# Two of eight feature blocks of the first token group change from eight full products to fourteen half-width ones

## The chip, the cores and the metric

The kernel runs on one core of a Trainium2 chip. Its time is the device time in microseconds (us) of one execution; the median of eight executions is given. Five engines work beside each other, each with its own queue of instructions that it takes in order: TensorE (PE in the profile, PEld its weight loads), VectorE (DVE), ScalarE (ACT), GpSimd (POOL) and the sync engine (SP), which issues most of the DMAs. They wait for each other through semaphores.

## The reference

Inputs are q, k, v of shape (8 batches, 8 heads, 576 positions, 64) and the weights w1, w2 (512 x 1024), w3 (1024 x 1024), w_out (1024 x 512), all float32.

```python
q_s = softmax of q over the last axis
k_s = softmax of k over the positions
kv  = einsum('bhsd,bhse->bhde', k_s, v)
x   = einsum('bhsd,bhde->bhse', q_s, kv)      # then (4608 tokens, 512 features)
a, b = x @ w1, x @ w2
out = ((a * b) @ w3) @ w_out                  # (4608, 512)
```

## The kernel before

**Weights.** w3 and w_out stand next to each other with nothing between them, so `make_w3o` multiplies them once (W3O, 1024 x 512), with TensorE transposes of w3. `make_w12` casts w1 and w2 to float16 in halves of 512 columns (fh 0 and 1) and also makes the combined weights `wc` that the half products need.

**Attention**, batch by batch and in two halves of four heads (i = 0, 1): exponentials of k and q on ScalarE (`ke`, `qe`), v cast (`vc`), sums and reciprocals of q's rows on VectorE (`qr`, `qi`), normalization (`qn`), transposition of q (`qt`, by TensorE with a copy `qv` for batches 0 to 3, by DMA for 4 to 7), kv on TensorE (`kv`, nine rows of 64 positions summed), its normalization on VectorE (`kn`), and x transposed (`x`), cast from PSUM to the tile `xt` (`xc`).

**The feed-forward part** takes the 4608 tokens in eight groups of 512 and 640 by turns. Its first product, a and b for eight blocks of 128 of the 1024 features, is written in one of two ways:

- `plain`: a = x w1 and b = x w2 for all tokens of the group, four products of depth 128 each (tasks `pa0`, `pa1`, `pb0`, `pb1`, two products in each). a is cast to SBUF (`pac`), and VectorE multiplies b in PSUM by it (`pm`, L664).
- `wino`: [w1, w2] and x are cut into two by two parts, with the group's tokens in halves, and seven products of parts (tasks `x1` to `x4`, `v1`, `v2`, `w`, each two matmuls over half of the tokens, L712) replace eight, as in Strassen's method in Winograd's form. The price is additions: four combinations of x for the group (`tt1` to `tt4`, L689), three snapshots of PSUM for each block (`e1` to `e3`, L385), four VectorE operations that read PSUM (`k1` to `k4`, L736; `k3` already multiplies) and one SBUF product (`k5`, L763).

Group 0 has all eight blocks `plain`, the other groups all eight `wino` (`PLAINS`, L278). The second product, `s2`, multiplies each tile of 128 tokens of a*b by W3O, eight products of 512 columns in four tasks of two (L816), each task needing two of the eight blocks. The result is evicted (`s2e`, L789 and L791) and stored (`so`, L779).

**The order** is written out by hand. Every piece of work is a task, numbered in the order in which the program adds it. `ORDER` lists the numbers in the order in which they are issued, `SLOTS` says which physical tile each buffer takes (10 staging tiles `st` for loads, 8 PSUM banks `ps`), and `ENGS` which engine does a task that has a choice. `Steps.run` (L239) goes through them; a tuple such as `('ps', 0, 11)` issues that many filler products on a blank tile (L985). An engine issues its tasks strictly in this order, and a reused tile makes a task wait for the last reader of the tile's former content. There are 28 fillers: 11, 3 and 2 among the transposes of w3, and 2, 8 and 2 around the first products of batch 0.

Of the kernel before, what the change touches and what calls it, by code (L numbers as in the profile page):

```python
# [18 lines left out]
    ('ps', 0, 11), 12, 6, 0, 1, 2, 3, 14, 120, 96, 97, ('ps', 0, 3), 72, 98, 73, 121, ('ps', 0, 2), 74, 68,  # L19
    122, 75, 80, 99, 123, 8, 81, 4, 69, 5, 82, 76, 10, 124, 128, 9, 83, 7, 84, 129, 104, 100, 130, 13, 105,  # L20
    88, 11, 131, 106, 15, 89, 132, 70, 90, 107, 108, 16, 91, 112, 17, 77, 92, 19, 125, 144, 18, 113, 85,
    142, 114, 101, 143, 109, 115, 145, 133, 71, 20, 116, 146, 147, 117, 93, 78, 140, 21, 134, 126, 135, 86,
    127, 79, 110, 136, 94, 111, 137, 102, 95, 150, 152, 22, 162, 103, 148, 164, 118, ('ps', 3, 2), 151,
    154, 163, 138, 149, 153, 139, 168, 171, ('ps', 5, 8), 155, 169, 24, 170, 23, 156, 141, 87, 119, 25,
    172, 157, 173, 165, ('ps', 2, 2), 181, 166, 158, 180, 475, 159, 160, 167, 469, 161, 481, 174, 478, 176,
    175, 472, 182, 484, 466, 183, 487, 467, 26, 479, 468, 188, 488, 470, 473, 184, 471, 190, 485, 482, 486,
    476, 502, 189, 496, 185, 503, 474, 30, 490, 191, 504, 27, 480, 497, 28, 493, 477, 194, 491, 29, 489,
    508, 31, 492, 494, 483, 1382, 495, 1396, 202, 192, 499, 204, 1397, 203, 509, 498, 505, 200, 500, 205,
    511, 510, 501, 506, 214, 1403, 507, 512, 212, 206, 1404, 513, 207, 1389, 196, 215, 1390, 197, 1398,
    213, 1391, 40, 1405, 216, 34, 193, 1392, 217, 1383, 1393, 1399, 208, 1400, 1384, 201, 209, 199, 218,  # L30
    210, 219, 1385, 198, 186, 211, 32, 222, 177, 38, 223, 179, 178, 1386, 33, 220, 224, 1406, 221, 225, 36,
    1407, 226, 229, 232, 227, 230, 1408, 228, 235, 234, 231, 533, 233, 35, 237, 518, 236, 535, 1387, 519,
    563, 514, 534, 520, 37, 515, 548, 539, 42, 516, 549, 517, 522, 521, 564, 537, 552, 536, 538, 554, 523,
    553, 567, 540, 187, 525, 541, 524, 526, 555, 542, 578, 527, 528, 568, 545, 529, 556, 530, 570, 239,
    546, 593, 531, 558, 571, 547, 565, 557, 594, 569, 559, 573, 532, 579, 543, 244, 572, 560, 195, 544,
    597, 595, 574, 598, 575, 566, 246, 582, 550, 561, 608, 583, 596, 600, 623, 551, 601, 584, 576, 624,
    599, 562, 585, 256, 247, 1417, 577, 286, 627, 602, 1410, 245, 586, 242, 605, 609, 603, 240, 606, 1411,
    587, 588, 628, 607, 580, 604, 288, 612, 581, 630, 39, 625, 248, 631, 589, 590, 249, 1409, 613, 610,
    626, 629, 238, 591, 1418, 1388, 611, 614, 41, 615, 632, 1431, 43, 592, 616, 635, 241, 1395, 617, 633,
    618, 636, 254, 1394, 620, 634, 1432, 637, 280, 1402, 621, 1412, 243, 619, 1419, 1401, 622, 255, 1433,  # L40
    284, 252, 281, 257, 1434, 253, 1424, 258, 287, 250, 1435, 259, 1425, 298, 289, 1420, 296, 264, 251,
    265, 1421, 290, 1413, 283, 285, 266, 262, 267, 282, 260, 263, 1426, 291, 261, 44, 271, 268, 272, 273,
    306, 47, 270, 269, 277, 307, 45, 278, 1414, 297, 274, 657, 275, 279, 1427, 640, 308, 276, 294, 309,
    292, 658, 295, 672, 293, 644, 638, 642, 717, 639, 1428, 659, 299, 687, 641, 643, 661, 1430, 663, 673,
    660, 646, 662, 676, 48, 645, 647, 664, 300, 648, 1415, 677, 665, 649, 301, 702, 666, 650, 667, 49, 679,
    703, 668, 669, 1416, 680, 652, 651, 678, 670, 682, 52, 688, 654, 681, 706, 1437, 671, 655, 691, 718,
    302, 683, 707, 1423, 304, 656, 653, 692, 684, 721, 303, 305, 1429, 674, 685, 704, 694, 675, 722, 709,
    705, 693, 695, 686, 689, 724, 696, 732, 690, 725, 697, 699, 733, 698, 723, 708, 710, 700, 727, 711,
    1445, 701, 726, 736, 714, 728, 737, 712, 729, 715, 325, 738, 730, 739, 310, 713, 740, 1446, 716, 312,
    741, 734, 337, 719, 311, 742, 720, 747, 744, 735, 748, 749, 731, 745, 1438, 324, 743, 751, 753, 750,  # L50
    67, 752, 1439, 754, 1440, 755, 1441, 756, 757, 746, 1442, 759, 758, 316, 313, 1444, 317, 319, 314,
    1447, 760, 315, 1436, 320, 766, 321, 781, 318, 767, 1443, 1452, 328, 762, 796, 46, 811, 782, 763, 768,
    335, 761, 1453, 769, 770, 764, 1448, 771, 329, 783, 330, 785, 773, 765, 772, 55, 784, 774, 1454, 812,
    775, 776, 786, 1455, 331, 359, 787, 778, 1456, 1449, 815, 788, 777, 1450, 1466, 789, 779, 1459, 1422,
    797, 790, 816, 798, 780, 54, 800, 323, 332, 791, 799, 1451, 333, 793, 322, 792, 818, 1457, 826, 794,
    819, 1460, 336, 801, 817, 827, 1461, 820, 358, 1462, 795, 338, 821, 50, 803, 813, 334, 822, 804, 830,
    339, 802, 814, 831, 806, 340, 1463, 823, 1467, 805, 1468, 1464, 824, 841, 807, 833, 808, 825, 834,
    1469, 341, 809, 832, 842, 856, 810, 871, 835, 857, 858, 326, 836, 859, 843, 860, 837, 872, 838, 844,
    861, 327, 847, 875, 839, 845, 876, 1473, 846, 828, 1470, 848, 829, 863, 1472, 862, 849, 877, 864, 1465,
    878, 850, 851, 879, 865, 866, 1471, 853, 840, 881, 867, 868, 854, 342, 364, 880, 855, 343, 852, 366,  # L60
    873, 344, 363, 1474, 345, 53, 883, 869, 1475, 1458, 882, 346, 870, 352, 51, 347, 874, 1480, 348, 354,
    1481, 353, 1482, 884, 920, 886, 905, 921, 907, 885, 890, 906, 888, 922, 887, 891, 1483, 908, 1476, 889,
    1484, 894, 924, 1477, 1485, 895, 909, 935, 435, 925, 923, 892, 910, 59, 897, 893, 927, 898, 896, 936,
    912, 928, 362, 899, 926, 913, 911, 929, 900, 930, 914, 950, 60, 901, 902, 951, 915, 931, 939, 62, 917,
    916, 940, 1487, 56, 903, 942, 918, 1486, 904, 954, 943, 941, 955, 937, 944, 932, 373, 945, 938, 957,
    946, 1488, 958, 933, 1489, 365, 934, 952, 947, 367, 349, 355, 919, 1490, 350, 351, 356, 965, 948, 960,
    966, 1494, 953, 357, 995, 374, 969, 996, 1495, 371, 949, 1496, 368, 970, 956, 369, 57, 967, 361, 959,
    1497, 372, 1491, 999, 962, 972, 963, 1515, 973, 961, 980, 971, 968, 370, 981, 1516, 964, 1000, 974,
    975, 1498, 984, 375, 976, 1001, 376, 1002, 1479, 977, 1003, 1508, 978, 982, 1004, 1005, 985, 997, 409,
    1006, 1007, 987, 998, 360, 1501, 377, 1008, 986, 988, 1502, 983, 402, 1503, 1009, 989, 1478, 1504, 979,  # L70
    992, 1500, 1505, 990, 993, 378, 991, 1492, 379, 994, 1493, 1517, 381, 398, 1509, 380, 403, 1510, 382,
    391, 385, 384, 383, 1518, 393, 392, 386, 1014, 387, 1044, 407, 1010, 388, 1511, 389, 390, 66, 1015,
    1029, 1011, 58, 1016, 1030, 1046, 1013, 1017, 1045, 1031, 1018, 1519, 1032, 1059, 1033, 1019, 1035,
    1012, 1034, 1522, 1512, 1047, 1048, 1021, 1513, 1049, 1020, 1022, 1036, 1514, 1523, 1023, 1037, 1050,
    396, 1507, 1038, 1039, 1051, 1040, 64, 1041, 1052, 1524, 1521, 1042, 1060, 1054, 1043, 1026, 1520,
    1053, 1063, 1074, 65, 1055, 1064, 1089, 395, 1525, 408, 1061, 1075, 1066, 1062, 1024, 1067, 1078, 1027,
    1529, 1025, 1079, 1065, 1028, 1090, 1056, 1068, 400, 1069, 1530, 1057, 1526, 1071, 61, 1070, 1081, 394,
    401, 1527, 1093, 1080, 1094, 1091, 1072, 1076, 404, 1531, 1082, 1073, 1092, 1096, 1077, 1095, 405, 410,
    1097, 1104, 1532, 1105, 1083, 1119, 1533, 1098, 1099, 1084, 1120, 1108, 1085, 1101, 1058, 1109, 406,
    1123, 1102, 436, 1086, 1536, 1087, 1103, 1124, 1537, 1100, 399, 1506, 1111, 1088, 1126, 411, 1121,  # L80
    1112, 412, 397, 1550, 1122, 1110, 1127, 1114, 431, 1113, 1543, 1115, 1129, 430, 414, 437, 413, 415,
    1544, 433, 416, 1538, 417, 432, 1499, 1106, 1125, 434, 1107, 1116, 1528, 1551, 1128, 1535, 1552, 1117,
    1130, 1131, 1118, 418, 1132, 450, 419, 451, 1133, 420, 421, 452, 1545, 423, 438, 422, 1546, 453, 1136,
    1553, 1547, 439, 424, 1554, 1168, 425, 1138, 426, 1153, 1556, 1539, 440, 1154, 1134, 63, 1183, 1169,
# [167 lines left out]
def kernel(  # L252
# [11 lines left out]
    nc = tc.nc  # L264
# [754 lines left out]
```

## Time and profile before

| what | value |
|---|---|
| median of 8 runs | 234.67 us (233.38 to 236.15) |
| the profiled execution | 234.03 us, its span 232.2 us |
| granted TensorE clock | 1.000 |
| TensorE busy | 221.1 us, 95% |
| VectorE, ScalarE, GpSimd busy | 186.8, 140.9, 90.8 us |
| HBM read, written | 38.80, 9.44 MB |

The span runs from the first to the last instruction. The first 33 us make W3O and batch 0's attention; TensorE's first product of group 0 starts at 33.4, of group 1 at 59.05, and the last product of all at 227.0. A row of a group gives the engine, the operation, what it writes and reads, its count, busy us and mean ns of one; means of operations in a run overlap, so busy divided by count is less than the mean.

### The profile page before, as it was taken

How to read it: one execution, taken by the hardware profiler on the slowest of the kernel's cores; microseconds unless marked ns; L12 is line 12 of the kernel's file. 1: busy time of each engine (PE TensorE's matmuls, PEld its weight loads, DVE VectorE, ACT ScalarE, POOL GpSimd, SP SyncE). 2: the span in 40 equal slices, each digit the busy share in tenths (PEclk: the TensorE clock that was granted, in tenths of full speed). 3: DMA queues.
4: the chain of work that ended last, by engine and by line, in shares of the span. 5: the costliest groups of instructions: out<-in, count | busy, mean ns of one | idle time of the engine just before them, and what ended most of it. 6: DMA issues, size and time to landing. Idle time of an engine off the chain costs nothing.

```text
span 232.2 us, 5571 instructions
## 1 busy us (share of the span) xinstructions
PE 221.1 (95%) x2068; PEld 134.2 (58%) x2068; DVE 186.8 (80%) x457; ACT 140.9 (61%) x306; POOL 90.8 (39%) x81
## 2 busy tenths in 40 slices
PE   7879989998999989999999999999999999999991
PEld 2544544444676558766665766656665766566640
DVE  1443695998999979989988998899988998899930
ACT  2335765556798978768745847487898843515111
POOL 3113335638268787210573535420552502210300
PEclk9999999999999999999999999999999999999999
DMA  6999999879952949948886797859664753042535
GB/s 250 380 343 389 394 387 368 295 260 350 392 190 48 332 168 324 318 130 239 234 199 136 211 326 214 167 179 273 212 99 97 200 114 76 0 90 46 118 94 134
DMA packets 32732, 50.96 MB, mean 219 GB/s; under 512 B 11712, under 2 KB 11712, under 8 KB 32704
## 3 DMA queue, kind: packets, MB, share of 16 engines
q1 hardware_dynamic: 32304, 49.95, 69.2%
q10 hardware_dynamic: 400, 0.66, 1.2%
q8 instruction: 16, 0.26, 0.5%
q14 instruction: 12, 0.10, 0.2%
HBM read 38.80 MB, written 9.44 MB: 208 GB/s over the span
## 4 chain that ended last, share of the span: by engine, by line
PE 79%; DMA 8%; DVE 7%; POOL 2%; ACT 1%; issue 1%; SPq 1%; DVEq 0%; POOLq 0%
PE ps L712 42%; PE ps L816 22%; DMA st<-in_moe_w_dram 5%; PE ps L647 5%; PE ps L418 4%; DMA st<-in_v_dram 3%; PE ps L607 2%; PE ps L562 2%; DVE eq L520 2%; DVE ds L510 1%; DVE ab L664 1%; PE ps L536 1%; POOL eq L520 1%; SPq L332 1%; PE ps L406 1%
## 5 line engine op out<-in xcount | busy, mean ns | idle before, releaser
L736 DVE TENSOR_TENSOR cc<-ps,uu 128x320 f16<-128x320 f32 (+1 forms) x168 | 71.7, 455 | 7.4 <-PE ps L712 3.7
L816 PE MATMUL ps<-W3O,ab 128*128 128x512 f16 x288 | 77.3, 379 | 0.0
L385 ACT COPY uu<-ps 128x320 f32<-128x320 f32 (+1 forms) x144 | 54.1, 406 | 36.3 <-PE ps L712 25.7
L712 PE MATMUL ps<-tt,wc 128*128 128x320 f16 (+1 forms) x336 | 57.5, 288 | 0.2 <-ACT uu L385 0.2
L712 PEld LDWEIGHTS <-wc 128*128 128x128 f16 x448 | 43.5, 98 | 19.7 <-issue 0.5
L520 POOL TENSOR_TENSOR eq<-eq,ds 128x1152 f16<-128x1152 f16 x14 | 30.1, 2147 | 34.5 <-DVE ds L517 25.9
L712 PEld LDWEIGHTS <-w 128*128 128x128 f16 x336 | 32.1, 98 | 16.6 <-issue 0.8
L712 PE MATMUL ps<-xt,w 128*128 128x320 f16 (+1 forms) x224 | 39.7, 288 | 0.0
L763 POOL TENSOR_TENSOR ab<-cc,cc 128x320 f16<-128x320 f16 (+1 forms) x27 | 20.0, 750 | 47.9 <-DVE cc L736 47.8
L816 PEld LDWEIGHTS <-ab 128*128 128x128 f16 x288 | 27.0, 98 | 18.5 <-issue 0.7
L736 DVE TENSOR_TENSOR ab<-ps,cc 128x320 f16<-128x320 f32 (+1 forms) x56 | 25.1, 454 | 1.4 <-PE ps L712 0.2
L789 ACT ACTIVATE osb<-ps 128x512 f32<-128x512 f32 x29 | 17.2, 602 | 13.8 <-PE ps L816 13.8
L385 ACT CAST xt<-ps 128x512 f16<-128x512 f32 (+3 forms) x43 | 15.0, 407 | 14.0 <-PE ps L607 14.0
L510 DVE TENSOR_REDUCE ds<-eq 128x9 f32<-128x576 f16 x32 | 23.2, 742 | 0.1
L506 ACT ACTIVATE eq<-st 128x576 f16<-128x576 f32 x32 | 21.3, 686 | 2.6 <-DMA st<-in_q_dram 2.1
L712 PE MATMUL ps<-tt,w 128*128 128x320 f16 (+1 forms) x112 | 22.6, 288 | 0.0
L712 PE MATMUL ps<-xt,wc 128*128 128x320 f16 (+1 forms) x112 | 22.3, 288 | 0.0
L475 ACT ACTIVATE ek<-st 128x576 f16<-128x576 f32 x32 | 21.1, 685 | 0.6 <-ACT ek L475 0.6
L689 POOL TENSOR_TENSOR tt<-xt,tt 128x640 f16<-128x640 f16 (+1 forms) x6 | 7.8, 1297 | 22.9 <-DVE tt L689 14.4
L418 PE MATMUL ps<-ab,ab 128*128 128x512 f16 x64 | 15.0, 379 | 0.3 <-DVE ab L385 0.3
L385 POOL CAST v<-st 128x1152 f16<-128x1152 f32 x11 | 13.0, 1193 | 5.5 <-DMA st<-in_v_dram 5.5
L647 PE MATMUL ps<-xt,w 128*128 128x512 f16 x64 | 14.8, 379 | 0.0
(55 smaller groups left out, 198.6 us busy)
## 6 DMA issues: line engine op xcount, KB each, us to landing
st<-in_q_dram SPq DMA_DIRECT2D x16, 576.0 KB, 5.0
st<-in_v_dram SPq DMA_DIRECT2D x16, 576.0 KB, 6.8
st<-in_k_dram SPq DMA_DIRECT2D x16, 576.0 KB, 5.9
out_dram<-osb SPq DMA_DIRECT2D x67, 128.0 KB, 2.5
st<-in_moe_w_dram SPq DMA_DIRECT2D x16, 512.0 KB, 8.8
st<-in_moe_w_out_dram SPq DMA_DIRECT2D x4, 512.0 KB, 7.3
out_dram<-osb ACTq DMA_DIRECT2D x5, 128.0 KB, 2.7
qsT<-eq SPq DMA_TRANSPOSE x8, 3.2
```

Source lines behind the costliest of these rows:

```text
L385: {"DVE": nc.vector.tensor_copy, "POOL": nc.gpsimd.tensor_copy, "ACT": nc.scalar.copy}[eng](out=o, in_=i)
L418: nc.tensor.matmul(pp.tile, lhsT=wT.tile[:, gt * P:(gt + 1) * P], rhs=wo[i][1].tile[:, (gt % 2) * C:(gt % 2 + 1) * C], start=(gt == 0), st ...
L475: nc.scalar.activation(out=ek.tile[:, :, j, :], func=AF.Exp, in_=vk(bk.tile)[:, j].rearrange("p (r d) -> p r d", r=RK))
L506: nc.scalar.activation(out=eq.tile[:, :, j, :], func=AF.Exp, in_=vq(bq.tile)[:, j].rearrange("p (r d) -> p r d", r=RK))
L510: nc.vector.tensor_reduce(out=ds.tile[:, 0, j], axis=AX.X, op=ALU.add, in_=eq.tile[:, :, j, :])
L520: {"POOL": nc.gpsimd, "DVE": nc.vector}[e].tensor_tensor(out=eq.tile, in0=eq.tile, op=ALU.mult, in1=ds.tile[:, 1].rearrange("p j r -> p r ...
L647: nc.tensor.matmul(ps.tile[:, 0:m], lhsT=w[qt][:, ct, fo:fo + P], rhs=x[:, ct, lo:lo + m], start=(ct == 0), stop=(ct == 3))
L712: nc.tensor.matmul(ps.tile[:, 0:h], lhsT=lhs(c), rhs=rhs(c), start=first and c == 0, stop=c == 1, skip_group_check=not first)
L736: return lambda: nc.vector.tensor_tensor(out=dst(), in0=ps.tile[:, 0:h], in1=other.tile[:, 0:h], op=op)
L763: {"POOL": nc.gpsimd, "DVE": nc.vector}[e].tensor_tensor(out=ab.tile[:, 0:h], in0=c11.tile[:, 0:h], in1=c21.tile[:, 0:h], op=ALU.mult)
L789: nc.scalar.activation(out=o(), in_=i(), func=AF.Copy, scale=ISC)
L816: nc.tensor.matmul(po.tile[:, :w], lhsT=rows(ab_buf[(g, ft)].tile), rhs=W3O[:, ft, m * w:(m + 1) * w], start=(ft == 0), stop=(ft == N_FT - 1))
```

## The change

Blocks 6 and 7 of group 0 go from `plain` to `wino`, with 256 tokens in each half. Group 0 so gets the four combinations of x too. This shifts the numbers of all later tasks, and `ORDER`, `SLOTS` and `ENGS` are written anew for the whole program. Some helpers gain cases that are not used here: `JB` is now asked for with the input's name and half, and a list `XTAIL` is added; both are empty.

```diff
-    ('ps', 0, 11), 12, 6, 0, 1, 2, 3, 14, 120, 96, 97, ('ps', 0, 3), 72, 98, 73, 121, ('ps', 0, 2), 74, 68,
...
+    ('ps', 2, 17), 14, 2, 8, 0, 1, 4, 10, 3, 104, 80, 81, 72, 128, 73, 82, 105, 68, 5, 129, 74, 6, 12, 130,
...
+    168, 171, ('ps', 4, 11), 170, 173, 152, 154, 153, 169, 155, 188, 156, 167, 95, 157, 490, 25, 172, 181,
...
-    PLAINS = {0: (0, 1, 2, 3, 4, 5, 6, 7)}
+    PLAINS = {0: (0, 1, 2, 3, 4, 5)}
...
     JB = []
+    XTAIL = []
...
-        if b in JB:
+        if (x, b, i) in JB:
...
+            if b in XTAIL:
+                pieces = [(0, 8)]
```

Read back into names (for a product task: name, group, block; for `s2`: group, tile, step; for attention: batch, half), the new order has these stretches. TensorE from the first fillers on, in the order before and in the new one (w3m, the W3O products, left out between):

```
before: 11 fillers, w3t 3, 3 fillers, w3t 0, w3t 6, 2 fillers, ... qt 0 0, kv 0 0, qt 0 0, 2 fillers, x 0 0, 8 fillers, kv 0 1, 2 fillers, qt 0 1, pb0 0 1, ...
new:    17 fillers, w3t 1, w3t 0, w3t 4, w3t 7, ... qt 0 0, qt 0 0, kv 0 0, kv 0 1, x 0 0, 11 fillers, pa0 0 4, pa0 0 5, qt 0 1, qt 0 1, pb0 0 1, pb0 0 0, x 0 1, pb0 0 2, pa0 0 1, pa0 0 0, pa0 0 2, pa1 0 4, pa1 0 5, pa1 0 0, ...
```

TensorE, new, from the first half product of group 0 to batch 2's kv:

```
x1 0 6, x1 0 7, pb1 0 2, pb0 0 3, w 0 7, pb1 0 3, pa0 0 3, s2 0 3 0, pa1 0 3, pb0 0 5, pb1 0 5, pb0 0 4, w 0 6, pb1 0 4, x2 0 7, x2 0 6, s2 0 0 0, x3 0 7, s2 0 0 1, v1 0 7, x3 0 6, s2 0 3 1, v1 0 6, x 0 1, x4 0 6, s2 0 3 2, s2 0 0 2, x4 0 7, v2 0 6, v2 0 7, six s2 0, qt 1 0, qt 1 0, four s2 0, kv 1 0, kv 1 1, qt 1 1, qt 1 1, four x 1, x1 1 0, 22 more tasks of group 1, kv 2 0, kv 2 1, ...
```

VectorE from its first operation on group 0's products to batch 1's first cast to xt:

```
before: pm 0 0, pac, wc1 0, pac, pac, pm, pm, pm, pm, wc0 1, qr 1 0, pac, qr 1 0, pm, pm, qi 1 0, pm, qr 1 1, qr 1 1, qi 1 1, wc1 1, qn 1 1, three qv, kn, kn, s2e, xc 1 0
new:    pac 0 0, pm 0 0, wc0 0, tt2 0, pm, pm, e1 0 7, wc1 0, wc0 1, wc2 1, wc1 1, pm, pm, k1 0 7, pm, k1 0 6, qr 1 0, k2 0 6, k2 0 7, qr 1 0, k3 0 6, qi 1 0, k3 0 7, k4 0 7, qr 1 1, qr 1 1, k4 0 6, k5 0 7, k5 0 6, qi 1 1, qv, s2e, qv, s2e, s2e, kn, kn, qv, xc 1 0
```

In the new order GpSimd makes `tt3 0`, `tt4 0`, two of the combined weights of half 1 and 0, and both normalizations of batch 1. The sync queue's loads of batches 2 and 3 and its first stores:

```
before: k3 half 0, k2, q2, q3, q2, v2, store, k2, store, v2, v3, q3, store, store, k3 half 1, v3 half 1, ...
new:    k2, q2, v2, k2, v2, q2, v3 half 1, store, k3 half 0, store, k3 half 1, v3 half 0, q3, q3, store, ...
```

## The prediction

> **What bounds the kernel now.** I read the page's busy line first, then ten-microsecond windows, then the chain of work that ended last, and last the groups kept apart by shape, for prices. The busy line and four windows (columns: window, its length, then busy us and instructions of PE, PEld, DVE, ACT, POOL, then granted clock, DMA share, GB/s):
>
> ```profile
> PE 221.1 (95%) x2068; PEld 134.2 (58%) x2068; DVE 186.8 (80%) x457; ACT 140.9 (61%) x306; POOL 90.8 (39%) x81
> 40.00:50.00 10.00, 10.00 (x48) 4.51 (x46) 9.28 (x17) 6.87 (x11) 3.91 (x4) 1.00 0.87 322
> 50.00:60.00 10.00, 8.89 (x140) 4.95 (x139) 8.83 (x18) 5.37 (x15) 6.92 (x3) 1.00 0.87 302
> 60.00:70.00 10.00, 10.00 (x74) 6.96 (x72) 9.61 (x23) 8.58 (x21) 5.70 (x5) 1.00 0.70 260
> 80.00:90.00 10.00, 9.05 (x219) 6.09 (x218) 8.62 (x27) 8.38 (x21) 7.68 (x6) 1.00 0.70 251
> ```
>
> TensorE is the bound: full in most windows, at the full clock. It has holes in two places, 50 to 60 us (1.1 us idle) and 80 to 90 us (0.95 us idle), and the chain (start, length, what) says what is late there:
>
> ```profile
> 45.12 0.69 DVE ab L664
> 45.81 0.60 DVE wc L436
> ...
> 52.73 2.22 DVE eq L520
> 55.08 0.66 PE ps L536 x9
> ...
> 59.12 10.78 PE ps L712 x78
> ...
> 75.31 7.57 DMA st<-in_v_dram
> 83.00 1.14 POOL v L385
> 84.15 2.12 POOL eq L520
> 86.31 0.68 PE ps L536 x9
> ```
>
> So group 0's stretch is not TensorE's alone. From 45 to 55 us the chain runs on VectorE, which has the products of group 0 (L664), the weight combinations (L436) and batch 1's softmax in one queue; only at 59.05 does group 1 start. And at 83 us a load of v, issued at 75.3 and landed at 83.0, holds batch 3's attention.
>
> **The prices.**
>
> ```profile
> L736 DVE TENSOR_TENSOR cc<-ps,uu 128x256 f16<-128x256 f32 x72 | 28.0, 417 | 3.1 <-PE ps L712 1.7 <-issue 0.4 <-ACT uu L385 0.2
> L763 DVE TENSOR_TENSOR ab<-cc,cc 128x256 f16<-128x256 f16 x15 | 4.1, 282 | 0.0
> L664 DVE TENSOR_TENSOR ab<-ps,cc 128x512 f16<-128x512 f32 x8 | 5.3, 686 | 2.8 <-PE ps L647 2.7
> ```
>
> Busy over count is what one costs in a run of them: 28.0/72 = 0.39 us, 4.1/15 = 0.27, 5.3/8 = 0.66. For TensorE I take start to start in the order of time: the 44 products of 512 columns from 35.34 to 44.85 give 0.216 us each, and in the chain 30 products of 256 columns take 3.28 us, 0.109 each.
>
> **1. Matmuls.** Blocks 6 and 7 lose 8 products of 512 columns each and get 14 of 256: 16 x 0.216 = 3.46 us goes, 28 x 0.109 = 3.05 us comes, **-0.41 us**. The added weight loads (98 ns) fit under 109 ns. This counts only where TensorE sets the pace; the two blocks lie in the stretch that ends with VectorE, so I book it there.
>
> **2. VectorE between group 0 and group 1.** I count its queue from its first operation on group 0's products to batch 1's first xt cast, in both orders. Before: 8 L664 5.3, 4 casts 2.7, 3 weight combinations 2.0, 4 sums 2.9, 2 reciprocals 0.5, 1 normalization 1.8, 3 qsT copies 1.4, kv2 work 0.9, 1 eviction 0.7, in all **18.2 us**; it really took 19.0 (39.5 to 58.5), 1.04 times the rows. After: 6 L664 4.0, 1 cast 0.7, 5 combinations 3.3 (two come from POOL's side), 8 reads of half products 3.1, 2 SBUF products 0.55, 1 snapshot 0.4, 1 xt combination 0.45, the same sums, reciprocals, copies and kv2 work 5.7, 3 evictions 2.0, no normalization (POOL has it): **20.2 us**, by the same 1.04 some 21. In the new order it can begin at about 38.5: TensorE's first product of group 0 was at 33.4, and eleven pairs of products (0.43 each) and about 0.4 us of transposes and x products stand ahead. So batch 1's xt casts fall near 59.6, and group 1 starts 1 us late. Lower end: the gaps close and TensorE alone decides, -0.4. Upper end: VectorE begins at 39.5 as now, +2.1. The added wait is on PSUM: the second transpose of batch 1 now takes the bank that block 6's last VectorE read frees, and behind it in TensorE's queue stand group 0's last second products and batch 1's kv. POOL's normalization of batch 1 (L520 is 2.15 us on POOL against 2.2 on VectorE in the chain) still begins after VectorE's reciprocal, so moving it frees VectorE but makes nothing earlier. I take **+0.9**.
>
> ScalarE also gets 3 us more up to there (three weight casts, one product cast, five snapshots of blocks 6 and 7, two qsT copies, against three copies of transposed weights and two evictions that leave it). It was busy 5.4 of 10 us at 50 to 60, which covers it; uncovered, it would delay batch 1's exponentials by that much, and the upper end above would move with it.
>
> **3. The beginning.** 28 filler products before and after, but 17 now stand ahead of the first weight transpose and none between the transposes. The row:
>
> ```profile
> 1.19 4.88 PE L985 MATMUL ps<-blank 128*128 128x512 f16 x11 [1.19 <-DVE blank L978]
> ```
>
> 0.43 us each up to 6.8 us, then 0.216: 17 end near 7.6 us. The first transposed block is now the one that POOL casts second (its casts end at 5.24 and 8.40 today), about 9.4 us, so TensorE pauses 1.8 us where its longest pause now is 1.1. [...] The trace shows the clock rising once and no pause long enough to test a fall. I take **0**: TensorE has 17.4 us of W3 x Wout work and both orders can finish near 27.5.
>
> **4. Batch 2's kv moves forward**, from behind group 1's products into their middle, after 23 pairs of group 1. Those take 23 x 0.272 = 6.3 us. Ahead of its second half ScalarE has nine snapshots (0.40), two exponentials of q and three of k (0.66 each): 6.9 us, begun half a microsecond later. TensorE waits about 1 us in a stretch that has no hole today; 0 to 1.2, I take **+0.8**, since one snapshot may slip into the wait.
>
> **5. Batch 3's loads move forward** on the sync queue: today its last k and v are issued at 74.6 and 75.3, behind stores. Now the four of k and v stand ahead of all stores but two, and wait only for staging slots that batch 1 and 2 free by about 65 us. The hole at 83 to 86 us (steps of 0.2, 0.5, 0.3 and 0.8 us over the usual, 1.8) should close; the windows count 0.95 idle. I take **-1.3**.
>
> **6. The rest.** After group 1's start VectorE has about 4 us less to do, ScalarE about 2 more, with the same TensorE work; the holes there are 0.2 to 0.5 us each and some 3 us in all, and I can say of none whether it stays: 0, with 1 us either way. The last eviction goes from ScalarE (0.60) to VectorE (0.68): **+0.1**. The JB and XTAIL edits run nothing (both lists are empty).
>
> **Sum**: 0.9 + 0 + 0.8 - 1.3 + 0 + 0.1 = +0.5 us, on the profiled execution 234.03 (span 232.2 and 1.8 around it) 234.5. The median of the runs is 0.64 above that execution, so the median becomes **235.2**. About 0.5% (1.2 us) is what a measurement of this kernel can tell from no change, so that is no change.
>
> **Rivals.** *VectorE takes the lead* (slower): step 2 at its upper end, 0.9 becoming 2.1 us, gives 235.2 + 1.2 = **236.4**. For it: VectorE is busy 9.28 and 8.83 of 10 us where the two blocks come in. Against: its queue starts a little earlier. It decides from the point where VectorE's first product of group 0 is later than about 38.9, or its queue to batch 1's casts longer than 21.5 us. *TensorE stays the bound* (faster): group 1 starts 0.4 us early, no wait at the kv, the hole at 83 closes: -0.4 - 1.8 + 0.1 = -2.1, **232.6**. For it: 95% busy and the late v load in the chain; against: the 45 to 55 us chain on VectorE. *The products change nothing* is inside my forecast's case: -0.41 us in a stretch that waits anyway.
>
> **How the numbers follow.** Forecast 0.43 (its own range 234.0 to 236.0, of which 0.40 lies within 0.5% of 234.67 and 0.03 above), VectorE 0.34, TensorE 0.23. With a little of each rival inside 0.5%: faster 0.21, same 0.44, slower 0.35. Range 232.8 to 237.2: the faster case's 232.6 with its spread loses half at the low end, the slower case takes another 0.8 us from steps 3 and 6.
>
> **What would show it.** TensorE 2080 instructions; batch 1's xt casts at 59 to 60 and the first product of group 1 at about 60; a TensorE wait on ScalarE near 66; no v load in the chain at 75 to 83. I am wrong if group 1 starts by 58.7 or after 61.2, if fillers and transposes give a half-clock stretch, or if holes of over 1 us appear after 90 us.

## The result, and the profile after

The changed kernel's median is 232.99 us (231.59 to 236.13) against 234.84 us (233.32 to 239.77) for the kernel before beside it: ratio 0.9925, 95% interval 0.9905 to 0.9945. The forecast was no change, at 235.2 us. The nearest case is the rival called "TensorE stays the bound", which had 232.6.

The profiled execution of the changed kernel took 234.26 us (span 232.5), no faster than the profiled one of before (234.03, span 232.2). That is not a contradiction but half of the finding. The 32 executions that were timed, with those of a later run of the same kernel, fall into two groups with nothing between: 18 from 231.59 to 233.11 us (middle 232.3) and 14 from 233.76 to 236.13 (middle 234.4). The profiled one is of the upper group. The mean granted clock of each execution goes with them: the 18 have 0.995 to 1.000, and 13 of the 14 have 0.985 to 0.993 (the other has 0.995). So two things are to be explained: why the lower group is 2.5 us faster than the kernel before, and what costs the upper group 2.1 us.

Four marks on TensorE cut an execution into parts. The table has each profiled execution; e1 to e7 are the experiments below. All times are us; the last two columns are the last matmul's start and the span.

| kernel | first product of group 0 | first product of group 1 | stretch between | group 1 to last matmul | last matmul | span |
|---|---|---|---|---|---|---|
| before | 33.39 | 59.05 | 25.66 | 167.94 | 226.99 | 232.2 |
| after | 34.49 | 60.32 | 25.83 | 167.23 | 227.55 | 232.5 |
| e1, 28 fillers first | 33.13 | 58.41 | 25.28 | 167.24 | 225.65 | 230.6 |
| e2, 11 fillers first | 34.02 | 59.30 | 25.28 | 167.28 | 226.58 | 231.5 |
| e3, plain products in the new order | 32.65 | 58.39 | 25.74 | 167.37 | 225.76 | 230.7 |
| e4, old order with early loads | 34.27 | 59.93 | 25.67 | 166.77 | 226.71 | 231.9 |
| e5, after once more | 34.84 | 60.42 | 25.58 | 167.22 | 227.64 | 232.6 |
| e6, 20 fillers first | 33.08 | 58.35 | 25.28 | 167.23 | 225.58 | 230.5 |
| e7, 24 fillers first | 32.58 | 57.85 | 25.28 | 167.22 | 225.07 | 230.0 |

The busy line of the changed kernel, which answers the first line shown of before, has the 2080 matmuls that were forecast, 12 more than before:

```profile
PE 221.9 (95%) x2080; PEld 137.2 (59%) x2080; DVE 186.9 (80%) x456; ACT 143.0 (62%) x318; POOL 93.5 (40%) x86
```

The same windows as before (window, its length, busy us and instructions of PE, PEld, DVE, ACT, POOL, granted clock, DMA share, GB/s):

```profile
40.00:50.00 10.00, 10.00 (x57) 5.33 (x55) 8.44 (x16) 7.24 (x13) 3.76 (x3) 1.00 1.03 385
50.00:60.00 10.00, 9.55 (x145) 5.53 (x146) 9.62 (x26) 8.79 (x17) 6.33 (x4) 1.00 0.75 257
60.00:70.00 10.00, 10.00 (x143) 6.76 (x143) 9.79 (x27) 8.50 (x22) 6.73 (x6) 1.00 0.66 219
80.00:90.00 10.00, 10.00 (x153) 6.38 (x151) 9.36 (x25) 7.94 (x20) 7.44 (x7) 1.00 0.68 224
```

Three things differ. The hole at 80 to 90 us is gone (9.05 to 10.00). The one at 50 to 60 has shrunk (8.89 to 9.55), although VectorE is busier there (8.83 to 9.62). And 60 to 70, where I expected TensorE to wait for ScalarE, is full. The chain of work that ended last (start, length, what) says the same:

```profile
60.34 6.55 PE ps L742 x46
66.90 0.79 PE ps L565 x72
67.69 2.69 PE ps L742 x18
...
80.03 1.29 PE ps L846 x6
81.32 0.22 PE ps L539 x4
81.55 2.59 PE ps L846 x12
...
221.88 6.06 PE ps L846 x28
...
227.97 0.69 DVE osb L821
```

L742, L565 and L846 are the half products, the kv and the second products (L712, L562 and L816 before). Batch 2's kv starts at 66.90 straight after the products ahead of it, and no load stands in the chain. What the changed kernel loses is at its very beginning. These are two of its windows of five us:

```profile
5.00:10.00 5.00, 2.54 (x9) 0.85 (x7) 0.78 (x1) 0.00 (x0) 2.02 (x2) 0.97 0.93 356
10.00:15.00 5.00, 4.97 (x46) 4.27 (x47) 3.79 (x6) 2.06 (x2) 1.04 (x1) 0.69 1.04 395
```

TensorE does half of a window's work from 5 to 10 us, and from 10 to 15 the granted clock (the number before the last two) is 0.69. In the clock's records it rises at 6.30, falls to half at 9.71 and rises again at 13.13. In the profiled execution of the kernel before it rose once, at 6.75, and stayed until after the last matmul. (Of the 58 executions of the kernel before that ran beside the experiments, seven have a mean clock of 0.992 or less, and all seven lie above their median.)

### The profile page after: what moved, and what is told of

The parts are those of the page before. It is cut to its first block, busy times and chain, and to the rows that moved or that the text cites. A ratio compares the mean times of both kernels' runs of the same rounds, so it can differ in the third digit from the quotient of the medians.

```text
span 232.5 us, 5615 instructions
## 1 busy us (share of the span) xinstructions
PE 221.9 (95%) x2080; PEld 137.2 (59%) x2080; DVE 186.9 (80%) x456; ACT 143.0 (62%) x318; POOL 93.5 (40%) x86
## 4 chain that ended last, share of the span: by engine, by line
PE 89%; DVE 4%; DMA 3%; POOL 1%; SPq 0%; issue 0%; ACT 0%
PE ps L742 44%; PE ps L846 26%; PE ps L421 6%; PE ps L677 4%; PE ps L612 3%; DMA st<-in_moe_w_dram 3%; PE ps L409 2%; PE ps L565 2%; PE ps L539 1%; DVE osb L821 1%; POOL ab L388 1%; DVE eq L523 1%; DVE ds L513 1%; DVE kv L576 1%; DVE qsT L388 1%; SPq L335 0%
## 5 line engine op out<-in xcount | busy, mean ns | idle before, releaser
L766 DVE TENSOR_TENSOR cc<-ps,uu 128x320 f16<-128x320 f32 (+1 forms) x174 | 73.8, 452 | 7.1 <-PE ps L742 2.4
L846 PE MATMUL ps<-W3O,ab 128*128 128x512 f16 x288 | 76.1, 379 | 0.0
L742 PE MATMUL ps<-tt,wc 128*128 128x320 f16 (+1 forms) x348 | 58.7, 287 | 0.0
L742 PEld LDWEIGHTS <-wc 128*128 128x128 f16 x464 | 44.1, 98 | 22.3 <-issue 0.8
L793 POOL TENSOR_TENSOR ab<-cc,cc 128x320 f16<-128x320 f16 (+1 forms) x30 | 22.5, 755 | 57.5 <-DVE cc L766 57.4
L742 PEld LDWEIGHTS <-w 128*128 128x128 f16 x348 | 33.6, 98 | 15.6 <-issue 1.1
L742 PE MATMUL ps<-xt,w 128*128 128x320 f16 (+1 forms) x232 | 41.2, 287 | 0.0
L846 PEld LDWEIGHTS <-ab 128*128 128x128 f16 x288 | 27.6, 98 | 18.8 <-issue 0.8
L819 ACT ACTIVATE osb<-ps 128x512 f32<-128x512 f32 x27 | 16.3, 608 | 17.4 <-PE ps L846 17.4
L388 ACT CAST xt<-ps 128x64 f16<-128x64 f32 (+3 forms) x50 | 17.5, 411 | 10.5 <-PE ps L612 10.2
L742 PE MATMUL ps<-tt,w 128*128 128x320 f16 (+1 forms) x116 | 23.0, 287 | 0.0
L742 PE MATMUL ps<-xt,wc 128*128 128x320 f16 (+1 forms) x116 | 22.7, 287 | 0.0
L388 DVE COPY uu<-ps 128x320 f32<-128x320 f32 (+1 forms) x29 | 13.0, 451 | 3.4 <-PE ps L742 3.0
L719 POOL TENSOR_TENSOR tt<-xt,tt 128x512 f16<-128x512 f16 (+1 forms) x5 | 6.4, 1272 | 20.3 <-ACT uu L388 13.5
```

The source lines that it names most:

```text
L388: {"DVE": nc.vector.tensor_copy, "POOL": nc.gpsimd.tensor_copy, "ACT": nc.scalar.copy}[eng](out=o, in_=i)
L742: nc.tensor.matmul(ps.tile[:, 0:h], lhsT=lhs(c), rhs=rhs(c), start=first and c == 0, stop=c == 1, skip_group_check=not first)
L766: return lambda: nc.vector.tensor_tensor(out=dst(), in0=ps.tile[:, 0:h], in1=other.tile[:, 0:h], op=op)
L793: {"POOL": nc.gpsimd, "DVE": nc.vector}[e].tensor_tensor(out=ab.tile[:, 0:h], in0=c11.tile[:, 0:h], in1=c21.tile[:, 0:h], op=ALU.mult)
L819: nc.scalar.activation(out=o(), in_=i(), func=AF.Copy, scale=ISC)
L846: nc.tensor.matmul(po.tile[:, :w], lhsT=rows(ab_buf[(g, ft)].tile), rhs=W3O[:, ft, m * w:(m + 1) * w], start=(ft == 0), stop=(ft == N_FT - 1))
```

## Experiments

The first four ran on one chip beside 29 executions of the kernel before (median 234.31 us), the last three on one chip beside 29 others (234.58). Each was profiled once.

**e1, more fillers ahead of the first transpose.** One number of the changed kernel's order is different:

```diff
-    ('ps', 2, 17), 14, 2, 8, 0, 1, 4, 10, 3, ...
+    ('ps', 2, 28), 14, 2, 8, 0, 1, 4, 10, 3, ...
```

> The changed kernel with 28 filler products instead of 17 ahead of the first weight transpose; nothing else. In the profiled execution of the changed kernel TensorE pauses 2.5 us (7.5 to 10.0), the granted clock is half from 9.7 to 13.1 us and 32 transposes take 3.4 us. Over its executions the ones with a mean clock of 0.993 or less lie near 234.3 us, the others near 232.6. Clock theory: the eleven added fillers (11 x 0.216 = 2.4 us) fill the pause, no execution loses the clock, all lie near 232.6 us, about 2.2 us under the kernel before (ratio about 0.990). Rival, loads set the start: the half clock lies under weight loads that arrive until 20 us, the added fillers change nothing, 233.0 us and the same spread.

Measured: 232.32 us (231.56 to 232.50, 6 executions), ratio to before 0.9890 [0.9845, 0.9936]. All six lie in the changed kernel's lower group, at mean clocks of 0.995 or more; in the profile the clock rises at 6.59 and holds until the matmuls end. Eleven needless products more make the kernel some 0.7 us faster in the medians. Its windows of the disputed stretch, and its chain there:

```profile
40.00:50.00 10.00, 10.00 (x62) 5.52 (x61) 9.85 (x20) 7.10 (x14) 3.29 (x2) 1.00 1.02 385
50.00:60.00 10.00, 9.55 (x146) 5.72 (x145) 9.62 (x27) 9.05 (x20) 6.38 (x3) 1.00 0.89 309
```

```profile
43.98 1.73 PE ps L677 x8
...
50.96 2.59 PE ps L846 x12
53.55 0.52 PE ps L539 x9
54.06 0.02 issue
54.09 0.49 DVE qsT L388
54.58 0.63 DVE osb L821
...
57.59 0.84 PE ps L612 x16
58.43 1.68 PE ps L742 x11
```

From 40 to 50 us VectorE is busy 98% of the time and still TensorE waits for nothing: the chain is TensorE's until 54.06, second products of group 0 (L846) filling the time until batch 1's normalized q is there. Only the last 3.5 us before the first x products (L612) run on VectorE.

**e2, fewer fillers**: the same number set to 11.

> The changed kernel with 11 filler products instead of 17 ahead of the first weight transpose: the pause grows from 2.5 to about 4 us. Clock theory: the clock falls in every execution, all lie near 234.3 us, ratio about 0.998. Rival, loads set the start: 233.0 us as the changed kernel.

Measured: 233.95 us (233.25 to 236.09, 12 executions), ratio 0.9981 [0.9945, 1.0018]. All twelve are above the changed kernel's lower group. In the profile the clock rises at 6.33, after the last filler has ended, falls at 9.74 and is back at 13.15. Nothing else in the order differs between e1 and e2, so the fillers at the start decide between the two groups. One thing doesn't fit the expectation that the clock falls every time: ten of the twelve have a mean clock of 0.985 to 0.993, but two, at 233.59 and 234.43 us, have 1.000. The clock's records begin with its first rise (in the profiles a window ahead of it reads 1.00, while products take 0.43 us there), so a rise that came only after the pause would look like this; neither of the two was profiled.

**e3, the new order with plain products.** Blocks 6 and 7 of group 0 are plain again; their eight products, two casts and two VectorE products stand where the half products stood, the combinations of x for group 0 and the snapshots are gone, and 28 fillers come first.

```diff
-    ('ps', 2, 17), ...
+    ('ps', 2, 28), ...
-    PLAINS = {0: (0, 1, 2, 3, 4, 5)}
+    PLAINS = {0: (0, 1, 2, 3, 4, 5, 6, 7)}
```

> The new order (with the 28 fillers of the first run, so that the clock plays no part), but blocks 6 and 7 of group 0 by eight full products again: pa0, pa1, pb0, pb1 stand where x1, w, x2, x3 stood, the other half products, the snapshots and the x combinations of group 0 are gone. To be compared with the first run. TensorE theory: TensorE is the bound in the stretch, and the half products are worth their 0.41 us: 0.4 us slower than the first run. VectorE theory (the prediction's step 2): VectorE sets the end of the stretch and has about 3 us less to do here, so group 1 starts about 1 us earlier: 1 us faster than the first run.

Measured: 232.99 us (232.47 to 233.38, 12 executions), ratio 0.9923 [0.9894, 0.9952]. Against e1 that is 0.67 us more in the medians. The table's stretch between the groups has 25.74 us for e3 and 25.28 for each of e1, e6 and e7: the half products are worth 0.46 us, and with plain products the new order is as long there as the old one (25.66). (In e3 the first transpose of batch 1, at 53.36, waits 0.05 us for GpSimd's normalization, so 0.41 of the 0.46 is TensorE's own.) All twelve executions lie in one group, at mean clocks of 0.995 or more. The half products gain although they put more work on VectorE, so VectorE does not set that stretch up to 54 us. e3's chain shows why: where e1 has half products it has plain ones, and from then on the two run alike:

```profile
44.14 3.45 PE ps L677 x16
...
49.90 3.56 PE ps L846 x16
53.46 0.58 PE ps L539 x9
54.05 0.02 issue
54.07 0.49 DVE qsT L388
```

e3's stretch has begun 0.48 us earlier (32.65 against 33.13) and arrives at this place at the same time.

**e4, the kernel before with batch 3's k and v loaded earlier.** Its second k and v loads go ahead on the sync queue, from behind the stores to the places behind the other v load and behind batch 2's q; one of them takes another staging tile. Nothing else changes; lines are names of tasks.

```diff
  v 3 0
+ k 3 1
  ...
  q's exponential 2 0 1
+ v 3 1        (staging tile 5 in place of 6)
  ...
- k 3 1
  ...
- v 3 1
```

> The kernel before, all full products, with two loads of batch 3 (half 1 of k and of v) taken ahead of the load of q half 1 on the sync queue, and v's staging slot changed from 6 to 5, so that v is issued near 68 us instead of 75.3. Hole theory: TensorE's hole at 83 to 86 us comes from this load; it closes and the time falls by about 1 us (0.95 idle by the windows), to 233.8. Rival: GpSimd, which casts v and then normalizes q (1.14 and 2.12 us in the chain), holds it in any case: less than 0.3 us.

Measured: 233.44 us (232.29 to 234.37, 12 executions), ratio 0.9967 [0.9938, 0.9995]. The two loads are issued at 62.95 and 69.17 us in place of 74.62 and 75.31, and this window of e4 answers the 9.05 of before:

```profile
80.00:90.00 10.00, 10.00 (x228) 6.95 (x227) 9.46 (x29) 9.32 (x22) 8.48 (x7) 1.00 0.63 191
```

From group 1 to the last matmul e4 takes 1.17 us less than the kernel before (167.94 to 166.77); the medians differ by 0.87. The late loads were the cause of the hole: the rival, that GpSimd holds it in any case, had less than 0.3 us.

**e5, e6 and e7: the length of the pause.** e5 is the changed kernel once more, e6 has 20 fillers and e7 24 in place of 17.

> The changed kernel itself again, beside two versions with a shorter pause at the start. Clock theory (the granted clock is settled once per stretch of 3.41 us, and falls when TensorE was idle for some 2.1 us or more of that stretch; how the stretches lie against the pause differs from one execution to the next): the pause is about 2.5 us, so some 45 in 100 executions lose 1.7 us; the executions lie in two groups, near 232.5 and near 234.3, and the median is 232.6 to 233.8. Rival, that the higher times are chance and not the clock: one group, with times that don't go with the mean clock.

> The changed kernel with 20 filler products at the start for 17, so that the pause is about 1.8 us, as the prediction had put it. Clock theory: 1.8 us is under 2.1, so no execution loses clock at the start; median 232.4, first product of group 0 near 33.2 us. Rival, that the chance of a fall only grows evenly with the pause (45 in 100 at 2.5 us, 83 in 100 at 3.5, so 20 in 100 at 1.8): two or three executions of a dozen near 234.2, median still 232.5. If half or more fall, the pause that the prediction expected would have cost as much as the real one.

> The changed kernel with 24 filler products at the start for 17: pause about 1.0 us, as the longest of the kernel before. Both theories: no fall, median 232.3, within 0.2 us of the 28 fillers' 232.32. If it is over 232.8, the extra fillers themselves, and not the missing pause, made the earlier gain.

Measured: e5 232.74 us (231.76 to 234.56), ratio 0.9925 [0.9891, 0.9959], five of twelve in the upper group; e6 232.59 us (231.64 to 234.37), 0.9913 [0.9883, 0.9944], two of twelve above 234; e7 232.19 us (231.59 to 235.11), 0.9906 [0.9871, 0.9940], two of twelve above 234 and one at 233.68. So e5 bears the clock theory out, but for e6 and e7 my estimate, that a fall needs some 2.1 us of idle time (the changed kernel's trace has 2.17 in the stretch ahead of its fall, 7.54 to 9.71) and that 1.8 is harmless, predicted none. The even growth with the pause (two or three of twelve) came nearer for e6; for e7 neither had any.

The profiles show what was missing. In these rows of TensorE (start, span, what, count, idle time before) the changed kernel, e5 and e6 follow in this order:

```profile
1.19 6.35 PE L1015 MATMUL ps<-blank 128*128 128x512 f16 x17 [1.19 <-DVE blank L1008]
10.03 3.42 PE L409 MATMUL ps<-ident,ab 128*128 128x128 f16 x32 [2.49 <-POOL ab L388]
```

```profile
1.19 5.13 PE L1015 MATMUL ps<-blank 128*128 128x512 f16 x17 [1.19 <-DVE blank L1008]
10.12 3.29 PE L409 MATMUL ps<-ident,ab 128*128 128x128 f16 x32 [3.80 <-POOL ab L388]
```

```profile
1.19 6.23 PE L1015 MATMUL ps<-blank 128*128 128x512 f16 x20 [1.19 <-DVE blank L1008]
9.79 2.06 PE L409 MATMUL ps<-ident,ab 128*128 128x128 f16 x32 [2.37 <-POOL ab L388]
```

The same 17 fillers end at 7.54 us in one execution and at 6.32 in another, because they run at 0.43 us each until the clock rises and at 0.216 after, and the clock rises anywhere from 3.84 (e5) to 7.15 us (e7). So a number of fillers does not fix the pause, and e6's was 2.37 us and not 1.8. Nor does the pause's length decide: 2.49 us was followed by a fall in the changed kernel and 2.37 by none in e6. All changes of the clock in these traces come 3.41 us, or a multiple of it, after the first rise. Measured by such stretches, TensorE's busy share was:

| kernel | clock rises at | stretch | busy share | clock at its end |
|---|---|---|---|---|
| e2 | 6.33 | 6.33 to 9.74 | 11% | falls |
| e5 | 3.84 | 3.84 to 7.25 | 73% | stays |
| e5 | | 7.25 to 10.67 | 16% | falls |
| after | 6.30 | 6.30 to 9.71 | 36% | falls |
| e6 | 4.75 | 8.16 to 11.57 | 52% | stays |
| e4 | 4.01 | 7.43 to 10.84 | 52% | stays |
| e4, last matmuls | | 225.88 to 229.29 | 35% | falls |
| e1, last matmuls | 6.59 | 225.05 to 228.46 | 29% | falls |

The e5 rows are the telling ones: around a pause of 3.80 us (6.32 to 10.12), longer than a stretch, the clock stayed at the end of the first stretch (73%) and fell at the end of the second (16%). Cut in this way from the first rise on, the nine traces hold 588 stretches at full clock: all ten with a share of 36% or less ended in a fall, and none of the 578 others, which begin at 52%, did. What a share between the two would bring, these traces don't show. Where the pause lies against the stretches differs between executions, and so does the outcome. This reading was formed after these runs.

If the same cuts are carried back ahead of the first rise, a stretch with 75% of work ended without a rise in e7 (0.32 to 3.73 us), and one with 78% ended with it in e5 (0.43 to 3.84). e2's eleven fillers take 4.88 us, 1.43 stretches; where they fell in two parts of under 75% each, the clock would by these two stretches rise only after the pause. That may be the two executions of e2 at 1.000, but it is an estimate from these shares and not shown.

e6's and e7's four executions above 234 us all have a mean clock of 0.993, and their twenty others 0.995 or more, so the four did lose clock. The reading would let them be those with an early rise, where the fillers end earliest; none of them was profiled, so the place of the fall stays open.

e7 and e1 beat both the kernel before and the changed one; their medians, 232.19 and 232.32, are not told apart.

## Why the prediction was wrong, by its own steps

**1, matmuls: right.** -0.41 us forecast, -0.46 measured (25.74 to 25.28, e3 against e1), of which 0.05 is e3's wait for GpSimd. But I booked it "in the stretch that ends with VectorE", as hidden, and there it is fully paid out. The margin was small: in e1 GpSimd's normalization ends at 53.28, 0.1 us before TensorE comes to it. The new order alone gives that stretch nothing (25.74 against 25.66).

**2, VectorE between group 0 and group 1: the step that failed.** I took +0.9 us; in e1, e2, e6 and e7 the stretch is 25.28 us against 25.66, **-0.38**. From VectorE's first operation on group 0's products to batch 1's first cast to xt I had 20.2 us by the rows, "some 21". In e1 it takes 18.4 (39.55 to 57.93), against 19.0 before. It also began 1 us later than the forecast's 38.5, and still ended 1.7 us ahead of the forecast's 59.6. Two errors:

- The price. I took busy over count, 0.66 us for an operation of 512 columns and 0.39 for a PSUM read of 256. In e1 such operations follow each other every 0.60 and 0.33 us. About 15 of the one and 9 of the other make 1.4 us. For TensorE I had counted start to start, for VectorE I had not.
- The factor 1.04, by which I scaled rows to reality, was no slowness of VectorE. Within those 19.0 us VectorE stood waiting for TensorE three times (VectorE's rows of the kernel before, the wait in brackets):

```profile
45.12 0.69 DVE L664 TENSOR_TENSOR ab<-ps,cc 128x512 f16<-128x512 f32 x1 [0.54 <-PE ps L647]
55.56 0.82 DVE L385 COPY qsT<-ps 128x640 f16<-128x640 f16 x2 [0.22 <-PE ps L536]
57.09 0.17 DVE L572 RECIPROCAL rc<-ps 128x2 f32<-128x2 f32 x1 [0.71 <-PE ps L562]
```

That is 1.47 us, so its work was 17.5 us and not more than the rows' 18.2. In e1 such waits are 0.27 us in all: the queue got 0.6 us more work and lost 1.2 us of waiting. Part of the queue that I called the bound was waiting for what it was said to hold up. The chain on VectorE from 45 to 55 us held TensorE's holes of 1.1 us, no more; in the new order second products of group 0 fill the wait for batch 1's q.

So the added VectorE work had room, and with the bound the sign of the step was wrong. In the profiled execution of the changed kernel group 1 starts at 60.32, near the forecast's 60, but by luck: 1.1 us of it stand before the first product of group 0. The stretch behind it is 0.55 us longer than in e1, and 0.30 in e5: by as much as VectorE's normalization of batch 0's second half takes longer there (1.90 and 1.65 us against 1.35 in e1, e2, e6 and e7). Why it does is not shown.

**3, the beginning: wrong in a way that has both signs.** I booked 0 for a pause of 1.8 us. The pause was 2.49 us in the profile, since the cast that ends it ended at 9.98 us and not near 9.4, and 3.80 in e5's, and the clock fell in 14 of 32 executions by the two groups. The three traces with a fall reach group 0 at 34.02 (e2), 34.49 and 34.84; e1, e3, e6 and e7, without one, at 32.58 to 33.13; the old start did so at 33.39 and 34.27 (e4). By their means (34.45, 32.86, 33.83) a fall costs 1.6 us, and the new start without one gains 1.0 on the old one, where single traces of one start differ by 0.5 to 0.9. (The groups lie 2.1 us apart; the longer stretch of step 2, in two of the three traces with a fall, can hold the rest.) I had no term for that gain. Which of the moved tasks brings it, these runs don't show; e1's chain there waits for batch 0's last v load (landed at 28.14) and then for VectorE's sums, not for TensorE.

That such a pause costs nothing, and the part that this step has in the 0.8 us of the range, were my estimates, and no run shows them: in the trace of before the clock rises at 6.75 and falls only at 232.03, after the last matmul. In their place the runs showed a fall at 9.71 us in the changed kernel, after a stretch of 3.41 us in which TensorE was busy 36%, and 1.6 us as the price of a fall by the means above.

**4, batch 2's kv: wrong in size.** +0.8 forecast, about 0.1 measured: the chain shows no wait between 60.34 and 67.69. I had counted ScalarE's work rightly, nine snapshots and five exponentials ahead of the second half, but priced it at 6.9 us. In the trace it runs from 61.05 to 67.16, 6.1 us, and the half that needs its last result starts at 67.22. It is the same price error as in step 2: snapshots in a row take about 0.32 us each (three from 61.05 to 62.02) where I took 0.40, and exponentials about 0.6 (four in 2.42 us in e1) where I took 0.66. The wait that I forecast is there, but small: 0.10 us pass between the starts of the halves' last and first matmul (67.12 and 67.22), where the steps beside them take under 0.01.

**5, batch 3's loads: right in mechanism.** -1.3 us forecast; e4, which makes this part alone, measured -1.17 in its part of the trace and -0.87 in the medians. In the new order the stretch from group 1 on gains 0.71, so the rest of that order gives back about 0.46. Where, these runs don't show; I had booked 0 with 1 us either way.

**6, the tail: wrong sign.** +0.1 forecast. From the last matmul's start to the end it is 5.25 us before and 4.93 after, **-0.3**. The last eviction is longer on VectorE, as priced (0.69 against 0.60), but the last store moved with it, which I had not counted: ScalarE issued it before, at 228.03, and the end came 4.21 us later; the sync engine issues it in e1, at 226.78, and the end comes 3.80 us later.

The sum, for an execution in which the clock holds: -1.0 (start) - 0.38 (stretch) - 0.71 (after group 1) - 0.3 (tail) = -2.4 us, and the groups' middles differ by 2.5 (232.3 against 234.84). The terms come from single traces, so the agreement is good to about half a microsecond. With a fall: +0.6 at the start, about 0 in the stretch, and the same two gains, in all -0.4; measured -0.4 (234.4). The median of the mixture lies between, at 232.99. That it came close to the rival's 232.6 is partly luck: that rival had no clock fall, no gain at the start, and 1.8 us for the hole at 83 us, where the forecast itself had 1.3 and e4 measured 1.17.

## What to carry to other kernels

Price a queue by start to start times in a busy run of it, for every engine and not only for the one thought to be the bound, and take its waits out before scaling: a queue that is found to be longer than its work may be waiting for the engine that it is said to hold up. A chain through an engine says what was late once, not that work added there will lengthen it.

Before a pause at the beginning of a kernel, do not ask how long it is (2.49 us was followed by a fall of the clock here, 2.37 us by none), but how little work any stretch of 3.41 us laid over it can hold, with the earliest and the latest rise of the clock (3.84 and 7.15 us in these traces): stretches with 36% ended in a fall, with 52% in none. Here a few filler products too many cost nothing that could be told (28 against 24: 232.32 and 232.19 us), since batch 0's loads set the pace behind them; too few cost 1.6 us, in some executions and not in others, so one profile does not tell.

## What was unexpected of the hardware

In the changed kernel a TensorE pause of 2.49 us, which left 36% of work in the 3.41 us from 6.30 to 9.71, was followed by half the clock for the whole of the next 3.41 us: the first 32 transposes took 3.42 us where they take 2.06 at full clock (e6). And one order of instructions gave two groups of times 2.1 us apart. The first rise of the clock came anywhere between 3.84 and 7.15 us in nine traces; that its place decides the group is not shown, since both profiled executions of this order (rises at 6.30 and 3.84) lie in the upper one.
